# Reordering the last stage of a Fourier-mixing and gated-MLP kernel: kept operands loaded one by one, seven-product units behind other units, another PSUM bank for one block

## The chip, the cores and the metric

The kernel runs on one core of one Trainium2 chip. The metric is the time of one execution on the device in microseconds (us), and lower is better. Engines are named as the profile names them: PE is TensorE (PEld its weight loads), DVE is VectorE, ACT is ScalarE, POOL is GpSimd, SP is SyncE, which here only issues DMA transfers; SPq stands for its queue of such instructions.

## What is computed

Two branches read the same layer-normalised input of 2048 tokens by 640 features, and their outputs are added to the input:

```python
xn = _layernorm(x, axis=-1)
a = einsum("bsd,ed->bse", xn, dft_hid_re);  b = einsum("bsd,ed->bse", xn, dft_hid_im)
A = einsum("ts,bse->bte", dft_seq_re, a) - einsum("ts,bse->bte", dft_seq_im, b)
gate = einsum("bsd,df->bsf", xn, W_gate);   up = einsum("bsd,df->bsf", xn, W_up)
B = einsum("bsf,fd->bsd", gate * (gate > 0) * up, W_down)
return x + A + B
```

The gated branch has 1728 hidden features. All is float32.

## The kernel before

**Numbers.** Each float32 operand is split into a high and a low part, and a product is three matmuls, high by high, high by low, low by high (`mm3`, lines 138 to 140). Splitting (`split`, lines 132 and 133) costs an ACT copy for the high part and a DVE subtraction for the low one.

**Stages.** The sequence transform comes first, then gate and up, and last (`project`, about the final 300 us) the products with the hidden transform's and the down projection's weights, which are summed in the same banks. The change touches this last stage alone.

**The last stage.** The tokens are taken in two halves, q=1 first, then q=0, each of two chunks of 512 columns. Products are arranged as Strassen's seven (with Winograd's sums): B11, T1, T2, B22, T3, T4, B21 are their names. Each runs over seven units (`UNITS`, line 1153): three of the hidden transform (`hid`, blocks 0-1, 2-3, 4), four of the down projection (`f`, and `odd`, the block left over, which is unit 4). B21 has only units 2 and 4. A full unit has two 128-row blocks. T1 to T4 first subtract two raw operands on DVE (line 1267), then split; B11, B22 and B21 split what was loaded. B11, T1, B21 and B22 also split their weights; T2, T3 and T4 load weights that were split earlier (`wparts`). A unit has two outputs (banks `a`, `b` or `c`) and, in B11, T1, B21 and B22, a third: the odd block (`v1`, `v2`, `v3`), all in bank `fixed[4]`. When a product is through its units, `read` lets DVE add the banks to tiles `y` (line 1179), which are stored once all their parts are in.

**A second level.** Seven smaller products (`second_level`, named 1 to 7 and run in the order 1, 2, 5, 6, 3, 7, 4), each over three groups, replace one quarter of the blocks. They are the seven-product units, 21 in all. They read operands that are kept throughout: X of q=1 and Y of q=0, three tiles each (pool `quads`), loaded by `fetch`. Products 5, 6, 7 and 4 first add two kept operands on DVE (`plus`, line 1414). They use banks `fixed[5]`, `[6]` and `[7]`.

**Order.** `todo` is a list of units, each with a load, a preparation, a run and a read. `drive(4, 2)` goes through it: at step i it issues the preparation of unit i-2, the load of unit i, the read of unit i-5 and the run of unit i-4. PE, SP and POOL keep this order; each has one queue, in which an instruction that waits holds up all that follow. ACT and DVE are ordered by a planner when the program is built, at most about three units ahead (`in_turn`). What runs ahead is limited by buffers: three `cb` tiles (split operands, pool `ring2`), five `wt` tiles, four `wr` tiles and twenty `rw` tiles (raw operands). In the kernel before, all kept operands and three `y` tiles are loaded at place 14 of the list (`LOADS_AT`), which is between units 4 and 5 of T1, q=1, and from place 20 on one seven-product unit follows every second unit (`spread`, `SINCE`, `EVERY`).

Of the kernel before, what the change touches and what calls it, by code (L numbers as in the profile page):

```python
# [7 lines left out]
F32 = mybir.dt.float32  # L8
# [4 lines left out]
P = 128  # L13
S, D, F = 2048, 640, 1728
KD = D // P
CH = 512
# [19 lines left out]
B11, B12, B21, B22, T1, T2, T3, T4, X4 = range(9)  # L36
# [24 lines left out]
GROUPS = (("hid", 0, 2, 0), ("f", 0, 2, 2), ("f", 4, 1, 4))  # L61
# [4 lines left out]
def fnet_reglu_kernel(  # L66
# [15 lines left out]
    nc = tc.nc  # L82
# [21 lines left out]
    pqd = [dram_p.tile([2, P, KD, CH], F32, name=f"pq{c}") for c in range(NCHUNK)]  # L104
    hd = [dram_p.tile([NF, P, W2], F32, name=f"hd{q}") for q in range(2)]
# [29 lines left out]
    def mm3(ps, w, m, first, last, more=False):  # L135

        (wh, wl), (mh, ml) = w, m
        nc.tensor.matmul(ps, wh, mh, start=first, stop=False, skip_group_check=more)  # L138
        nc.tensor.matmul(ps, wh, ml, start=False, stop=False, skip_group_check=more)  # L139
        nc.tensor.matmul(ps, wl, mh, start=False, stop=last, skip_group_check=more)  # L140
# [12 lines left out]
    todo = []  # L153
    idle = lambda: None
# [637 lines left out]
    steps = [(q, i) for q in (1,) for i in range(SET_STEPS)]  # L792
# [48 lines left out]
    pool = open_pools.__getitem__  # L841
# [312 lines left out]
    ODD_AT, PARTS = 4, {"T2": Z2, "T3": Z3, "T4": Y22}  # L1154
    UNITS.insert(ODD_AT, ("odd", (0,)))
    SINGLE = (2, ODD_AT)
    LOADS_AT, SINCE, EVERY = 14, 20, 2
    every = range(len(UNITS))
    fixed = [bank() for _ in range(8)]
    y, missing, ends = {}, {}, []  # L1160
# [9 lines left out]
    def get_y(q, *which):  # L1170
        for e, c in which:
            own = f"{q}" if e in (0, 1, 4) and c == 0 else ""
            y[q, e, c] = t = pool("y").tile([P, CH], F32, name=f"y{e}{c}{own}")
            nc.sync.dma_start(t, xt[e * P : (e + 1) * P, (2 * q + c) * CH : (2 * q + c + 1) * CH])
# [18 lines left out]
    def project(q):  # L1193
# [1 line left out]
        raws = {}  # L1195
        A, Bk = (fixed[0:2], fixed[2:4]) if q else (fixed[2:4], fixed[0:2])
        B = {("a", 0): A[0], ("a", 1): A[1], ("b", 0): Bk[0], ("b", 1): Bk[1], ("c", 0): Bk[0], ("c", 1): Bk[1],
             "v1": fixed[4], "v2": fixed[4], "v3": fixed[4]}

        def get(kind, u):  # L1200
            what, ks = UNITS[u]
# [16 lines left out]
        def unit(name, u, first, last):  # L1218
            what, ks = UNITS[u]
# [89 lines left out]
            def run():  # L1309
                b, w = t["b"], t["w"]  # L1310
                key, o, row4 = {"B11": ("a", 0, (2 * P, "v1")), "T1": ("b", P, (0, "v2")), "B21": ("c", 0, (2 * P, "v3")),
                                "T2": ("a", 0, None), "B22": ("b", P, (0, "v2")), "T3": ("a", 0, None),
                                "T4": ("a", 0, None)}[name]
                more = name in ("T2", "B22", "T3", "T4")
                for out, oo in [((key, i), o + i * P) for i in range(2)] + ([(row4[1], row4[0])] if row4 else []):
                    if short:
                        for v in range(2):
                            nc.tensor.matmul(B[out], w[:, v, oo : oo + P], b, start=False, stop=last and v == 1, skip_group_check=more)  # L1318
                        continue
                    if (q, name, u, out) == (0, "T4", len(UNITS) - 1, ("a", 1)):  # L1320


                        add_y(0, 3, 0, B[out])
                        for half in range(2):
                            at, ps = slice(half * HC, (half + 1) * HC), fixed[5 + half][:, :HC]
                            for j in range(n):
                                mm3(ps, (w[:, j, 0, oo : oo + P], w[:, j, 1, oo : oo + P]), (b[:, 0, j, at], b[:, 1, j, at]),
                                    j == 0, j == n - 1)
                            ends.append((ps, half))
                        continue  # L1330
                    for j in range(n):
                        mm3(B[out], (w[:, j, 0, oo : oo + P], w[:, j, 1, oo : oo + P]), (b[:, 0, j], b[:, 1, j]),
                            first and not more and j == 0, last and j == n - 1, more)

            return load, prepare, run

        LOADS_Y = {"B11": ((0, 0), (1, 0), (4, 1), (4, 0)) if q else ((4, 1),), "T1": ((2, 1), (3, 1)), "T2": ((0, 1), (1, 1)), "T4": ((2, 0), (3, 0))}

        def read(name):
            two = range(2)  # L1340
            if name == "B11":
                todo = [(4, 1, "v1"), (4, 0, "v1")] + [(i, 0, ("a", i)) for i in two]
            elif name == "T1":
                todo = [(2 + i, 1, ("b", i)) for i in two]
            elif name == "B21":
                todo = [(i, 0, ("c", i)) for i in two] + [(4, 0, "v3")]
            elif name == "T2":
                todo = [(i, 1, ("a", i)) for i in two]
            elif name == "B22":
                todo = [(i, 1, ("b", i)) for i in two] + [(4, 1, "v2")]  # L1350
            elif name == "T3":
                todo = [(2 + i, 1, ("a", i)) for i in two]
            else:
                todo = [(2 + i, 0, ("a", i)) for i in two]
            for e, c, key in todo:
                if name == "T4" and q == 0 and e == 3:
                    for ps, j in ends:
                        add_y(q, e, c, ps, at=slice(j * HC, (j + 1) * HC), queue=(nc.scalar, nc.sync)[j])
                else:
                    add_y(q, e, c, B[key], late=q == 0 and name in ("T3", "T4"))  # L1360

        steps = []
        for name, us in (("B11", every), ("T1", every), ("T2", every), ("B22", every[:4]), ("T3", every),
                         ("B22", every[4:]), ("T4", every[:2]), ("B21", SINGLE), ("T4", every[2:])):
            whole = SINGLE if name == "B21" else every
            for u in us:
                l, p, r = unit(name, u, u == whole[0], u == whole[-1])
                steps.append((l, p, r, (lambda name: lambda: read(name))(name) if u == whole[-1] else idle))
                if u == (5 if (q, name) == (1, "B11") else 3) and name in LOADS_Y:
                    steps.append(((lambda which: lambda: get_y(q, *which))(LOADS_Y[name]), idle, idle, idle))  # L1370
        return steps

    def second_level():
# [2 lines left out]
        X, Y = {}, {}  # L1376
        a, x, v = fixed[5:]

        def fetch(g):
            what, k, n, _ = GROUPS[g]  # L1380
            for t, q in ((X, 1), (Y, 0)):
                t[g] = o = pool("quads").tile([P, 2 * n, CH], F32, name=f"q{q}{g}")
                if what == "hid":
                    nc.sync.dma_start(o, pqd[2 * q][1][:, k : k + 2 * n])
                else:
                    first = 2 * k + 1
                    nc.sync.dma_start(o, hd[q][first : first + 4 * n - 1 : 2, :, :CH].rearrange("f p t -> p f t"))  # L1387

        def unit(name, g):
            what, k, n, at = GROUPS[g]  # L1390
# [21 lines left out]
            def prepare():  # L1412
                lo, hi = halves
                plus = lambda o, i: nc.vector.tensor_tensor(o, o, i, op=OP.add)
                with in_turn():
                    src = {"1": X[g][:, lo], "2": X[g][:, hi], "5": X[g][:, lo], "6": X[g][:, lo], "3": Y[g][:, hi],
                           "7": Y[g][:, lo], "4": X[g][:, lo]}[name]
                    if name in "5674":
                        plus(src, {"5": Y[g][:, lo], "6": Y[g][:, hi], "7": Y[g][:, hi], "4": X[g][:, hi]}[name])
                    t["b"] = b = pool("ring2").tile([P, 2, SG, CH], F32R, name="cb")[:, :, :n]  # L1420
                    lows.append(split(b[:, 0], b[:, 1], src))
                    if "r" in t:
                        cs = slice(0 if block is not None else P, 2 * P if odd else P)
                        split(t["w"][:, :, 0, cs], t["w"][:, :, 1, cs], t["r"][:, :, cs])
# [16 lines left out]

            return load, prepare, run, read if g == len(GROUPS) - 1 else idle

        loads = [((lambda g: lambda: fetch(g))(g), idle, idle, idle) for g in range(len(GROUPS))]
        loads.append((lambda: get_y(0, (0, 0), (1, 0), (4, 0)), idle, idle, idle))
        return loads, [unit(name, g) for name in "1256374" for g in range(len(GROUPS))]

    def spread(steps, more, since, every_n):

        mixed, more = [], list(more)  # L1450
        for i, s in enumerate(steps):
            mixed.append(s)
            if i >= since and (i - since) % every_n == every_n - 1 and more:
                mixed.append(more.pop(0))
        assert not more, len(more)
        return mixed

    steps = project(1) + project(0)
    loads, quads = second_level()
    steps[LOADS_AT:LOADS_AT] = loads  # L1460
    todo.extend(spread(steps, quads, SINCE, EVERY))
    with tc.manual_schedule(engines={mybir.EngineType.SP, mybir.EngineType.Pool, mybir.EngineType.PE}):
        drive(4, 2)

# [38 lines left out]
```

## Time and profile before

| | us |
|---|---|
| median of three runs | 1039.2 (1038.14 to 1041.25) |
| the profiled execution | 1038.6 |
| its span, first to last instruction | 1036.8 |
| PE busy | 1020.4 |
| DVE busy | 837.1 |
| the three matmuls of `mm3` with `cb` and `wt` | 159.1, 159.3 and 158.8, 407 each |

The profile is of one execution. Its page gives the busy time of each engine, the span in 40 slices of 25.9 us (digits are tenths), the DMA queues, and the costliest groups of instructions. Other views used below: the list of who waited for whom (engine, line, what for; total us, times, longest), instructions in order of time (start, us, engine, line, operation; in brackets the idle time of the engine before and who ended it), windows (busy us and count of PE, PEld, DVE, ACT and POOL, then granted clock, DMA share and GB/s) and groups of instructions by line and shape (busy us, mean ns | idle before). Matmuls overlap, so a row's 0.39 us is not the distance to the next one. Rows of SPq are the issue of a transfer, not its time.

### The profile page before, as it was taken

The numbers are of one execution on the slowest core, as the hardware profiler recorded it, in microseconds if no ns is written. First come the engines' busy times: TensorE is split into PE (matmuls) and PEld (weight loads), VectorE is DVE, ScalarE is ACT, GpSimd is POOL, SyncE is SP. The second block draws the span as 40 slices with busy tenths as digits, with TensorE's granted clock in tenths as the row PEclk, the third lists the DMA queues.
The fourth block names the chain that finished last, engine by engine and source line by source line (L and its number), as shares of the span: only waits on it lengthen the run. The fifth ranks groups of instructions, "written<-read, shape, count | busy, mean of one in ns | idle before, by whom it ended". The sixth has DMA issues, their size and how long they took to land.

```text
span 1036.8 us, 12735 instructions
## 1 busy us (share of the span) xinstructions
PE 1020.4 (98%) x4510; PEld 842.3 (81%) x4510; DVE 837.1 (81%) x1178; ACT 458.5 (44%) x592; POOL 104.7 (10%) x171
## 2 busy tenths in 40 slices
PE   9999999999999999999999999999979999999998
PEld 8888888888888888888888888888867888787886
DVE  7967977969889697787878888885657889989777
ACT  6764453333334444333446444443524445554443
POOL 2000011112200002311100110111000001000001
PEclk9999999999999999999999999999998999999999
DMA  9884744958859566763464667653996586978775
GB/s 331 327 278 158 257 150 137 364 199 266 319 207 368 174 210 223 247 200 132 179 243 156 224 233 266 236 208 123 355 399 224 169 249 187 304 254 270 224 233 179
DMA packets 114767, 245.31 MB, mean 237 GB/s; under 512 B 12688, under 2 KB 63120, under 8 KB 112912
## 3 DMA queue, kind: packets, MB, share of 16 engines
q1 hardware_dynamic: 96320, 171.72, 50.1%
q0 software_dynamic: 17952, 72.36, 18.8%
q8 instruction: 35, 0.57, 0.2%
q10 hardware_dynamic: 432, 0.43, 0.1%
q14 instruction: 28, 0.23, 0.1%
HBM read 185.73 MB, written 57.69 MB: 235 GB/s over the span
## 4 chain that ended last, share of the span: by engine, by line
PE 91%; DMA 4%; DVE 3%; SPq 1%; issue 0%; ACT 0%; ACTq 0%; DVEq 0%
PE ps L140 29%; PE ps L139 29%; PE ps L138 29%; PE ps L526 3%; DMA wr<-in_wd 2%; DMA rw<-hd 1%; DVE cb L133 1%; PE ps L555 1%; DVE rw L1267 1%; DMA rw<-pq 1%; PE ps L1318 1%; PE ps L120 1%; DVE wt L133 0%; DMA ro<-hd 0%; SPq L1387 0%
## 5 line engine op out<-in xcount | busy, mean ns | idle before, releaser
L138 PE MATMUL ps<-cb,wt 128*128 128x512 f32 (+1 forms) x407 | 159.1, 391 | 8.3 <-ACT wt L132 7.6
L139 PE MATMUL ps<-cb,wt 128*128 128x512 f32 (+1 forms) x407 | 159.3, 391 | 3.2 <-DVE cb L133 3.2
L140 PE MATMUL ps<-cb,wt 128*128 128x512 f32 (+1 forms) x407 | 158.8, 390 | 0.1
L132 ACT ACTIVATE cb<-rw 128x1024 fp32r<-128x1024 f32 (+1 forms) x73 | 71.1, 976 | 99.2 <-PE ps L140 56.9
L132 ACT ACTIVATE cb<-raw 128x1024 fp32r<-128x1024 f32 x64 | 67.9, 1060 | 105.2 <-PE ps L140 97.0
L133 DVE TENSOR_TENSOR cb<-rw,cb 128x1024 fp32r<-128x1024 f32 (+1 forms) x73 | 81.5, 1118 | 29.8 <-ACT cb L132 29.5
L133 DVE TENSOR_TENSOR cb<-raw,cb 128x1024 fp32r<-128x1024 f32 x64 | 78.1, 1220 | 31.8 <-ACT cb L132 31.5
L138 PE MATMUL ps<-xs_early,gw 128*128 128x512 f32 x260 | 101.1, 389 | 0.0
L139 PE MATMUL ps<-xs_early,gw 128*128 128x512 f32 x260 | 101.1, 389 | 0.0
L140 PE MATMUL ps<-xs_early,gw 128*128 128x512 f32 x260 | 101.1, 389 | 0.0
L138 PEld LDWEIGHTS ps<-cb,wt 128*128 128x128 f32 x407 | 76.9, 189 | 25.0 <-ACT wt L132 8.1
L139 PEld LDWEIGHTS ps<-cb,wt 128*128 128x128 f32 x407 | 76.9, 189 | 21.1 <-DVE cb L133 5.2
L138 PE MATMUL ps<-cb,xs_late 128*128 128x512 f32 x232 | 90.2, 389 | 0.0
L139 PE MATMUL ps<-cb,xs_late 128*128 128x512 f32 x232 | 90.2, 389 | 0.0
L140 PE MATMUL ps<-cb,xs_late 128*128 128x512 f32 x232 | 90.2, 389 | 0.0
L140 PEld LDWEIGHTS ps<-cb,wt 128*128 128x128 f32 x407 | 76.8, 189 | 16.0 <-DVE wt L133 0.6
L138 PE MATMUL ps<-cb,xs_early 128*128 128x512 f32 x226 | 87.9, 389 | 0.0
L139 PE MATMUL ps<-cb,xs_early 128*128 128x512 f32 x226 | 87.9, 389 | 0.0
L140 PE MATMUL ps<-cb,xs_early 128*128 128x512 f32 x226 | 87.9, 389 | 0.0
L129 ACT ACTIVATE gw<-z 128x1024 fp32r<-128x1024 f32 (+1 forms) x52 | 57.0, 1112 | 36.5 <-PE ps L140 21.0
L129 ACT ACTIVATE u<-ps 128x512 f32<-128x512 f32 x52 | 31.2, 599 | 89.6 <-PE ps L140 77.7
L874 DVE TENSOR_TENSOR gw<-z,gw 128x1024 fp32r<-128x1024 f32 (+1 forms) x52 | 64.7, 1283 | 1.9 <-ACT gw L129 1.8
(208 smaller groups left out, 2034.9 us busy)
## 6 DMA issues: line engine op xcount, KB each, us to landing
raw<-in_dft SPq DMA_DIRECT2D x94, 512.0 KB, 5.6
wt<-wparts SPq DMA_DIRECT2D x70, 256.0 KB, 3.9
z<-in_wgu SPq DMA_DIRECT2D x26, 640.0 KB, 4.1
hd<-ob POOLq DMA_DIRECT2D x26, 512.0 KB, 3.2
wparts<-pw POOLq DMA_DIRECT2D x12, 1024.0 KB, 5.1
rw<-hd SPq DMA_DIRECT2D x24, 512.0 KB, 6.0
tk<-in_dft SPq DMA_DIRECT2D x16, 512.0 KB, 8.3
rw<-pq SPq DMA_DIRECT2D x16, 512.0 KB, 5.0
```

Of the source, the lines that this page charges most:

```text
L120: nc.tensor.matmul(ps[:, :P], warm, warm, start=True, stop=True)
L129: return nc.scalar.activation(o, i, AF.Copy)
L132: nc.scalar.activation(hi, src, AF.Copy)
L133: return nc.vector.tensor_tensor(lo, src, hi.bitcast(F32), op=OP.subtract)
L138: nc.tensor.matmul(ps, wh, mh, start=first, stop=False, skip_group_check=more)
L139: nc.tensor.matmul(ps, wh, ml, start=False, stop=False, skip_group_check=more)
L140: nc.tensor.matmul(ps, wl, mh, start=False, stop=last, skip_group_check=more)
L526: nc.tensor.matmul(E[0, key], xn_part(n * SG + j, d)[v == 1], b[:, int(v == 2), j], start=False, stop=n % NH == NH - 1 and (j, v) == (SG - ...
L555: nc.tensor.matmul(E[c, key], xn_part(j, d)[v == 1], b[c][0][:, int(v == 2), j], start=j == 0 and v == 0, stop=False)
L874: tt(self.w[:, 1, cs], self.z[:, cs], self.w[:, 0, cs].bitcast(F32), op=OP.subtract)
L1267: sub = lambda o, i0, i1: nc.vector.tensor_tensor(o, i0, i1, op=OP.subtract)
L1318: nc.tensor.matmul(B[out], w[:, v, oo : oo + P], b, start=False, stop=last and v == 1, skip_group_check=more)
```

## The change

The order of the last stage is written anew, and one bank moves:

- Kept operands and y tiles: `fetch` loads one tile at a time. The eight loads (X0, X1, X2, one y, Y0, Y1, Y2, two y) come one by one behind units 1, 3, 5 and 6 of T2, units 1, 3 and 5 of T3, and unit 2 of T4, all of q=1.
- The seven-product units stand one behind each unit of B22 of q=1, B11 of q=0 and B22 of q=0, seven each.
- For q=1, `v1` uses `fixed[7]` instead of `fixed[4]`. For q=0 it keeps `fixed[4]`, and the `v2` products of unit 0 of T1 are put behind the first output of unit 1.

```diff
-    LOADS_AT, SINCE, EVERY = 14, 20, 2
...
-             "v1": fixed[4], "v2": fixed[4], "v3": fixed[4]}
+             "v1": fixed[7 if q else 4], "v2": fixed[4], "v3": fixed[4]}
+        put_off = []
...
-                for out, oo in [((key, i), o + i * P) for i in range(2)] + ([(row4[1], row4[0])] if row4 else []):
+                each = [((key, i), o + i * P) for i in range(2)] + ([(row4[1], row4[0])] if row4 else [])
+                if (q, name, u) == (0, "T1", 0):
+                    put_off.append(each.pop())
+                for out, oo in each:
...
+                    if (q, name, u, out) == (0, "T1", 1, ("b", 0)):
+                        begin()
+                if put_off and (q, name, u) == (0, "T1", 0):
+                    out, oo = put_off.pop()
+                    put_off.append(lambda: [mm3(B[out], (w[:, j, 0, oo : oo + P], w[:, j, 1, oo : oo + P]), (b[:, 0, j], b[:, 1, j]),
+                                                j == 0, False) for j in range(n)])
+
+            begin = lambda: put_off.pop()()
...
-                steps.append((l, p, r, (lambda name: lambda: read(name))(name) if u == whole[-1] else idle))
+                step = [(l, p, r, (lambda name: lambda: read(name))(name) if u == whole[-1] else idle)]
                 if u == (5 if (q, name) == (1, "B11") else 3) and name in LOADS_Y:
-                    steps.append(((lambda which: lambda: get_y(q, *which))(LOADS_Y[name]), idle, idle, idle))
+                    step.append(((lambda which: lambda: get_y(q, *which))(LOADS_Y[name]), idle, idle, idle))
+                steps.append((step, (q, name, u)))
...
-        def fetch(g):
+        def fetch(t, q, g):
             what, k, n, _ = GROUPS[g]
-            for t, q in ((X, 1), (Y, 0)):
-                t[g] = o = pool("quads").tile([P, 2 * n, CH], F32, name=f"q{q}{g}")
...
+            t[g] = o = pool("quads").tile([P, 2 * n, CH], F32, name=f"q{q}{g}")
...
-        loads = [((lambda g: lambda: fetch(g))(g), idle, idle, idle) for g in range(len(GROUPS))]
-        loads.append((lambda: get_y(0, (0, 0), (1, 0), (4, 0)), idle, idle, idle))
+        alone = lambda f: (f, idle, idle, idle)
+        loads = [alone((lambda t, q, g: lambda: fetch(t, q, g))(t, q, g)) for t, q in ((X, 1), (Y, 0)) for g in range(len(GROUPS))]
+        loads.insert(3, alone(lambda: get_y(0, (4, 0))))
+        loads.append(alone(lambda: get_y(0, (0, 0), (1, 0))))
...
-    steps = project(1) + project(0)
     loads, quads = second_level()
-    steps[LOADS_AT:LOADS_AT] = loads
-    todo.extend(spread(steps, quads, SINCE, EVERY))
+    LOADS_AFTER = [(1, "T2", u) for u in (1, 3, 5, 6)] + [(1, "T3", u) for u in (1, 3, 5)] + [(1, "T4", 2)]
+    for q in (1, 0):
+        for steps, of in project(q):
+            todo.extend(steps)
+            if of in LOADS_AFTER:
+                todo.append(loads.pop(0))
+            if of[:2] in ((1, "B22"), (0, "B11"), (0, "B22")):
+                todo.append(quads.pop(0))
```

More of the change, by code (lines that the diff above doesn't have):

```diff
@@ L1377, in second_level @@
         a, x, v = fixed[5:]
-        def fetch(g):
+        def fetch(t, q, g):
             what, k, n, _ = GROUPS[g]
-            for t, q in ((X, 1), (Y, 0)):
-                t[g] = o = pool("quads").tile([P, 2 * n, CH], F32, name=f"q{q}{g}")
[L1383 to L1387, printed above, removed]
+            t[g] = o = pool("quads").tile([P, 2 * n, CH], F32, name=f"q{q}{g}")
+            if what == "hid":
+                nc.sync.dma_start(o, pqd[2 * q][1][:, k : k + 2 * n])
+            else:
+                first = 2 * k + 1
+                nc.sync.dma_start(o, hd[q][first : first + 4 * n - 1 : 2, :, :CH].rearrange("f p t -> p f t"))
         def unit(name, g):
@@ L1415, in prepare @@
                 with in_turn():
-                    src = {"1": X[g][:, lo], "2": X[g][:, hi], "5": X[g][:, lo], "6": X[g][:, lo], "3": Y[g][:, hi],
-                           "7": Y[g][:, lo], "4": X[g][:, lo]}[name]
+                    which, half = {"1": (X, lo), "2": (X, hi), "5": (X, lo), "6": (X, lo), "3": (Y, hi), "7": (Y, lo), "4": (X, lo)}[name]
+                    src = which[g][:, half]
                     if name in "5674":
-                        plus(src, {"5": Y[g][:, lo], "6": Y[g][:, hi], "7": Y[g][:, hi], "4": X[g][:, hi]}[name])
+                        which, half = {"5": (Y, lo), "6": (Y, hi), "7": (Y, hi), "4": (X, hi)}[name]
+                        plus(src, which[g][:, half])
                     t["b"] = b = pool("ring2").tile([P, 2, SG, CH], F32R, name="cb")[:, :, :n]
@@ L1442, in unit @@
             return load, prepare, run, read if g == len(GROUPS) - 1 else idle
-        loads = [((lambda g: lambda: fetch(g))(g), idle, idle, idle) for g in range(len(GROUPS))]
-        loads.append((lambda: get_y(0, (0, 0), (1, 0), (4, 0)), idle, idle, idle))
+        alone = lambda f: (f, idle, idle, idle)
+        loads = [alone((lambda t, q, g: lambda: fetch(t, q, g))(t, q, g)) for t, q in ((X, 1), (Y, 0)) for g in range(len(GROUPS))]
+        loads.insert(3, alone(lambda: get_y(0, (4, 0))))
+        loads.append(alone(lambda: get_y(0, (0, 0), (1, 0))))
         return loads, [unit(name, g) for name in "1256374" for g in range(len(GROUPS))]
[L1448 to L1456, printed above, removed]
-    steps = project(1) + project(0)
-    loads, quads = second_level()
-    steps[LOADS_AT:LOADS_AT] = loads
-    todo.extend(spread(steps, quads, SINCE, EVERY))
+    loads, quads = second_level()
+    LOADS_AFTER = [(1, "T2", u) for u in (1, 3, 5, 6)] + [(1, "T3", u) for u in (1, 3, 5)] + [(1, "T4", 2)]
[6 more added lines that the diff above has]
+                todo.append(quads.pop(0))
+    assert not loads and not quads
     with tc.manual_schedule(engines={mybir.EngineType.SP, mybir.EngineType.Pool, mybir.EngineType.PE}):
```

## The prediction

> **What bounds the kernel now.** I read the page first, then what TensorE waited for, then TensorE's instructions in order of time.
>
> ```profile
> span 1036.8 us, 12735 instructions
> ...
> PE 1020.4 (98%) x4510; PEld 842.3 (81%) x4510; DVE 837.1 (81%) x1178; ACT 458.5 (44%) x592; POOL 104.7 (10%) x171
> ...
> PE   9999999999999999999999999999979999999998
> PEclk9999999999999999999999999999998999999999
> ```
>
> TensorE is the bound: 98% busy. One slice, the 31st (777 to 803 us), stands out, and there the granted clock falls too. What it waited for over the whole span:
>
> ```profile
> PE ps L138 <- ACT wt L132: 7.6, 1, 7.6
> PE ps L139 <- DVE cb L133: 3.2, 3, 1.8
> ...
> PE ps L138 <- DVE y L1179: 0.6, 1, 0.6
> ```
>
> So five waits are all that an edit of the order can win. I place them by counting matmuls from 730.11 us, where unit 0 of B11, q=1, begins (18 matmuls for a unit of two blocks and three outputs, 12 for two outputs). Here are the first two of them:
>
> ```profile
> 757.08 0.39 PE L140 MATMUL ps<-cb,wt 128*128 128x512 f32 x1
> 758.09 0.50 PE L138 MATMUL ps<-cb,wt 128*128 128x512 f32 x1 [0.62 <-DVE y L1179]
> ...
> 769.10 0.39 PE L138 MATMUL ps<-cb,wt 128*128 128x512 f32 x1
> ...
> 771.60 0.39 PE L140 MATMUL ps<-cb,wt 128*128 128x512 f32 x1
> 779.62 0.80 PE L138 MATMUL ps<-cb,wt 128*128 128x512 f32 x1 [7.64 <-ACT wt L132]
> ...
> 784.75 0.39 PE L140 MATMUL ps<-cb,wt 128*128 128x512 f32 x1
> ```
>
> Eleven matmuls start from 769.10 to 771.60: 0.227 us each. At 758.09 stands T1, unit 0, third output (`v2`): 1.01 us after the one before, 0.78 lost. At 779.62 stands T1, unit 5. From 771.60 to 784.75 twelve matmuls start in 13.15 us where 2.72 would do: **10.4 us lost**, 7.8 by waiting and 2.6 by slow matmuls:
>
> ```profile
> 770.00:780.00 10.00, 2.36 (x10) 1.60 (x8) 2.36 (x2) 1.79 (x2) 0.00 (x0) 0.71 1.06 390
> 780.00:785.00 5.00, 4.92 (x13) 3.50 (x13) 5.00 (x6) 2.85 (x3) 0.00 (x0) 0.56 1.09 354
> 785.00:790.00 5.00, 5.00 (x24) 4.14 (x23) 4.29 (x6) 1.58 (x2) 0.00 (x0) 1.00 0.19 70
> ```
>
> The granted clock is 0.71, then 0.56, then 1.00 again. The wait is named for ACT, but ACT was itself late. I follow it back through VectorE to the transfers:
>
> ```profile
> 776.46 1.23 DVE L1267 TENSOR_TENSOR rw<-rw 128x1024 f32<-128x1024 f32 x1 [10.06 <-DMA rw<-hd]
> ```
>
> ```profile
> 755.20 1.01 SPq L1384 DMA_DIRECT2D q<-pq  x2
> 756.62 5.92 SPq L1387 DMA_DIRECT2D q<-hd  x4
> 762.59 2.20 SPq L1174 DMA_DIRECT2D y<-in_xt  x3
> 764.83 1.41 SPq L1216 DMA_DIRECT2D rw<-hd  x1
> ```
>
> ```profile
> 754.60:779.60 25.00, 16.76 (x73) 13.24 (x71) 12.62 (x17) 5.89 (x8) 0.00 (x0) 0.89 1.05 399
> ```
>
> The operand of T1, unit 5 (`rw<-hd`, 764.83) is issued behind the six kept operands and three y tiles, and the transfers are full all that time (399 GB/s, last column). The kept operands are four of 1.05 MB and two of 0.52, the y tiles three of 0.26: 6.0 MB, 15.1 us at 399 GB/s.
>
> **Part 1, the kept operands.** All nine transfers remain, but each now follows a unit of T2, T3 or T4. T1, unit 5 then is next in SP's queue at 755.2, and its operand, seen at 776.46, would land 15.1 us sooner, near 761.3. From its landing to the first matmul took 779.62 - 776.46 = 3.2 us; without a wait that matmul is due at 771.83. It must land by 768.6: 7.3 us to spare. So the wait goes, and with it the slow matmuls: **-10.4**.
>
> What is late next? The three operands of q=1 (X: 1.05, 1.05, 0.52 MB) fall into T2, the three of q=0 (Y, same sizes) into T3. The weight slices of both stages wait for one of five `wts` tiles, so SP cannot run far ahead. In T2 the tightest slices, those of unit 4, can go out when unit 0 ends, 6.8 us before they are used (30 matmuls); the operand ahead of them went out some 5 us earlier. Slices land in 3.5 us in the median (this row is of T3, q=0):
>
> ```profile
> wt<-wparts SPq DMA_DIRECT2D x12, 256.0 KB, 3.5
> ```
>
> So some 3 us are left: 0 for T2. T3 is tighter. It appears without extra transfers for q=0:
>
> ```profile
> 986.50:1002.80 16.30, 16.30 (x73) 13.49 (x72) 11.32 (x13) 8.67 (x11) 0.00 (x0) 1.00 0.80 247
> ```
>
> It moves 247 GB/s at a DMA share of 0.80, with TensorE never waiting. In q=1 the slices of T3, unit 1 wait for a tile that is freed 6.8 us before T3 begins; Y0 follows. From there to the end of unit 6's loads stand 6.7 MB: Y 2.6, operands and slices of units 2 to 6 4.1. Unit 6 starts 13.6 us into T3; less some 1.5 us to start a transfer, 17.9 us are there. At 399 GB/s the 6.7 MB take 16.8 us: no wait. At 247/0.80 = 309 GB/s they take 21.7: 3.8 us of wait. I take **+1.0**, nearer the full queue's row, which is the state that this stage would be in, and keep 0 and 3.8.
>
> How a wait is priced hangs on the clock. Two waits below, 1.76 us the longer, leave it at 1.00 in this trace; 7.64 us halved it. The Trainium skill, "TensorE: Matmul & The Clock Gate", section "HAM oscillation — how this bites in real kernels", says that idle gaps beyond about 3.4 us drop the clock and shorter ones don't; the trace agrees on both sides. By that rule a new wait of 3.8 us would cost 6.4, one of 3 us only itself.
>
> **Part 2, the bank.** For q=1 the odd block of B11 (`v1`) goes to bank 7 instead of bank 4, so T1's `v2` need not wait until VectorE has read `v1`: **-0.8**. Bank 7's former tenant is the last result of the gate-and-up rest, read by
>
> ```profile
> 730.94 0.68 DVE L989 TENSOR_TENSOR st<-ps,st 64x512 f32<-64x512 f32 x1 [0.75 <-ACT st L988]
> ```
>
> until 731.62, while `v1`'s first matmul comes 12 after 730.11, at 732.83. 1.2 us cover it; were that read later, each us beyond would be lost again. For q=0 six matmuls move behind the next unit's first six. Their number is unchanged and TensorE doesn't wait there now: 0. They hold one of three `cb` tiles 1.4 us longer; unit 3 begins 4.8 us after even the later release: covered.
>
> **Part 3, the seven-product units.** All 21 are kept, now behind each unit of B22 (q=1), B11 and B22 (q=0). Now they run from T2 of q=1 to T1 of q=0, where VectorE was late twice; a third such wait is in the last stage:
>
> ```profile
> 893.57 0.50 PE L139 MATMUL ps<-cb,wt 128*128 128x512 f32 x1 [1.76 <-DVE cb L133]
> ...
> 941.74 0.50 PE L139 MATMUL ps<-cb,wt 128*128 128x512 f32 x1 [0.92 <-DVE cb L133]
> ...
> 1030.28 0.50 PE L139 MATMUL ps<-cb,wt 128*128 128x512 f32 x1 [0.54 <-DVE cb L133]
> ```
>
> The first is T4, unit 5 of q=1, the second T1, unit 3 of q=0, the third T4, unit 6 of q=0. The first shows why:
>
> ```profile
> 891.16 1.22 DVE L1414 TENSOR_TENSOR q<-q 128x1024 f32<-128x1024 f32 x1
> 892.30 2.35 DVE L133 TENSOR_TENSOR cb<-rw,cb 128x1024 fp32r<-128x1024 f32 x2
> ```
>
> A sum for a seven-product unit stood ahead of the `cb` that TensorE needed. With no such unit among T1 to T4 both go: **-2.7**. T4 of q=1 then looks like T4 of q=0, which has none now and still waits: **+0.6** (0.54 and its restart; 0 to 1.8).
>
> But the units with the most sums (products 6, 7, 4) now meet B11 and B22 of q=0. The prices:
>
> ```profile
> L133 DVE TENSOR_TENSOR cb<-rw,cb 128x1024 fp32r<-128x1024 f32 x59 | 71.8, 1220 | 24.5 <-ACT cb L132 24.3
> ...
> L133 DVE TENSOR_TENSOR wt<-wr,wt 128x768 fp32r<-128x768 f32 x29 | 27.6, 951 | 1.9 <-ACT wt L132 1.9
> ...
> L133 DVE TENSOR_TENSOR cb<-q,cb 128x1024 fp32r<-128x1024 f32 x14 | 17.1, 1220 | 1.4 <-ACT cb L132 1.3
> ...
> L133 DVE TENSOR_TENSOR cb<-q,cb 128x512 fp32r<-128x512 f32 x7 | 4.8, 687 | 1.0 <-ACT cb L132 1.0
> ...
> L1414 DVE TENSOR_TENSOR q<-q 128x1024 f32<-128x1024 f32 x4 | 4.9, 1217 | 0.0
> ```
>
> A B11 or B22 unit costs VectorE 1.22 + 0.95 = 2.2 us for 4.1 of TensorE. Product 6 or 7 costs 1.22 + 1.22 = 2.4 for 1.4 (6 matmuls). Together 4.6 for 5.5: that fits. The crowded place is product 4 behind the last three units of B22, q=0:
>
> ```profile
> 1002.90:1021.20 18.30, 18.30 (x82) 15.16 (x81) 17.16 (x22) 7.61 (x10) 1.62 (x3) 1.00 0.68 208
> ```
>
> There VectorE has 1.1 us idle in 18.3 already. Product 4 adds about two units of 2.4 and one of 1.4, with small weight splits 7 us, for 15 matmuls, 3.4 us. That is 3.6 more work than time; less the idle 1.1, 2.5 late. T3 just before it has VectorE 5 us idle (11.32 of 16.30, quoted above), but work may be taken at most some three units ahead. Between 0 and 2.5, and with the last T4 losing its lead up to 3: **+1.5**.
>
> The sum: -10.4 - 0.8 - 2.7 + 1.0 + 0.6 + 1.5 = -10.8. The profiled execution took 1038.6 us (1036.8 of span, 1.8 around it), so 1027.8. It lies 0.6 under the median of the runs, 1039.2; I write **1028**.
>
> **Rivals.** (1) *The transfers' wait moves to T3 of q=1.* For it: 6.7 MB in 17.9 us need 374 GB/s, and T3's many 256 KB slices have not run at more than 247 on the mean. Against it: that stage was not full there, and full stretches show 399. At 309 GB/s 3.8 us and the halved clock's 2.6 take the place of my 1.0, at 285 5.6 and 2.6: 1033 to 1035. (2) *VectorE becomes the bound around q=0's B11 and B22.* For it: product 4's 2.5 us, and the order of VectorE's work is fixed beforehand, so that a wrong turn such as that at 891.16 costs 1 to 2 us wherever it falls. Against it: B11 and B22 leave it 1.9 us per unit. With the full 3 at the end and the 2.7 back in other places: 1032. (3) *The change doesn't do what it says*: T1, unit 5 is late even without the nine transfers, since transfers are full from 734 us on. Against it: 7.3 us to spare. With half of the 10.4 left: 1033. (4) *Slower:* rival 1's mechanism, at its extreme. Every transfer of SP is in one order, so Y in T3 delays the slices of all later units. It decides from 220 GB/s: then 6.7 MB take 30.4 us, 12.5 of wait and 2.6 of clock, which eat the 11.8 gained elsewhere and 3 more: 1042. Nothing seen in a full stretch is so low.
>
> **How the numbers follow.** Forecast 0.70, rival 1 0.14, rival 2 0.08, rival 3 0.05, rival 4 0.03. The forecast's own ends: no wait in T3, none new in the last stage, none in T4 of q=1 give 1024.7; a little less if the last stage's own wait shrinks too, 1024.3. All three at their bounds (3.8, 3 and 1.8) give 1033.3. I take 1024.3 to 1033.5, which also holds part of rivals 1 to 3. 0.3% is 3.1 us, about what a measurement of this kernel can tell from no change: faster 0.92, within 0.05, slower 0.03, since rivals 1 to 3 mostly stay beyond 3.1.
>
> **What would show it.** Right: T1, unit 5 without a wait, and the clock at 1.00 through the slice of 777 us; no wait on `y` at T1, unit 0; no wait at T1 of q=0. Wrong: a TensorE wait named for a slice (`wt`) or a DMA in T3 of q=1; VectorE without idle time and `cb` waits over 2 us after B22 of q=0; a wait in B11, unit 0 of q=1 for bank 7. If the clock falls anywhere, the forecast is too low.

## The result, and the profile after

| | before | after |
|---|---|---|
| median, us | 1039.82 (five runs, 1038.14 to 1041.38) | 1034.83 (five runs, 1034.15 to 1035.23) |
| the profiled execution, us | 1038.6 | 1035.23 |
| its span, us | 1036.8 | 1033.5 |

The ratio is 0.995, with a 95% interval of 0.9935 to 0.9964: faster by 5.0 us. The forecast was 1028.0, in a range of 1024.3 to 1033.5. The direction was right, about half of the gain came, and the time lies 1.3 us above the range.

The page of the changed kernel: span, the engines' busy time, and the 40 slices of TensorE and of its granted clock.

```profile
span 1033.5 us, 12722 instructions
...
PE 1020.2 (99%) x4510; PEld 840.5 (81%) x4510; DVE 837.8 (81%) x1178; ACT 457.5 (44%) x592; POOL 104.8 (10%) x171
...
PE   9999999999999999999999999999999989999997
...
PEclk9999999999999999999999999999999999999999
```

Both dips of before are gone: TensorE's own, which stood in the 30th slice (752 to 778 us) and not in the 31st as the prediction reads it, and the clock's in the 31st. A slight new one stands in the 33rd (827 to 853 us). What TensorE waited for (what for, who, total us, times, longest):

```profile
PE ps L139 <- DVE cb L133: 2.9, 5, 0.9
PE ps L138 <- DMA wt<-wparts: 2.1, 3, 1.5
PE ps L1321 <- DVE wt L133: 2.1, 2, 1.4
PE ps L140 <- DVE wt L133: 1.4, 1, 1.4
PE ps L120 <- DVE warm L116: 1.1, 1, 1.1
```

The one wait of 7.6 us has become many short ones, none above 1.5 us. The last row is the start of the program and was there before. Their places, from TensorE's instructions in order of time:

```profile
797.92 0.50 PE L140 MATMUL ps<-cb,wt 128*128 128x512 f32 x1 [1.35 <-DVE wt L133]
...
831.43 0.47 PE L138 MATMUL ps<-cb,wt 128*128 128x512 f32 x1 [0.35 <-DMA wt<-wparts]
...
833.30 0.47 PE L138 MATMUL ps<-cb,wt 128*128 128x512 f32 x1 [0.25 <-DMA wt<-wparts]
...
837.80 0.47 PE L138 MATMUL ps<-cb,wt 128*128 128x512 f32 x1 [1.51 <-DMA wt<-wparts]
...
842.17 0.74 PE L1321 MATMUL ps<-cb,wt 128*128 128x512 f32 x2 [1.37 <-DVE wt L133]
...
904.11 0.50 PE L139 MATMUL ps<-cb,wt 128*128 128x512 f32 x1 [0.77 <-DVE cb L133]
...
1018.69 0.50 PE L139 MATMUL ps<-cb,wt 128*128 128x512 f32 x1 [0.88 <-DVE cb L133]
...
1022.20 1.15 PE L1321 MATMUL ps<-cb,wt 128*128 128x512 f32 x4 [0.72 <-DVE wt L133]
...
1026.93 0.50 PE L139 MATMUL ps<-cb,wt 128*128 128x512 f32 x1 [0.56 <-DVE cb L133]
```

The first is B22, unit 0 of q=1, then T3, units 4, 5 and 6 of q=1, and B22, unit 4 of q=1; 904.11 is B11, unit 5 of q=0, and the last three are T4, units 3, 4 and 6 of q=0. Each wait costs a little more than its idle time, because the next matmuls start late too. So I add up, as the prediction did, what each start-to-start distance has over 0.227 us (those above 0.30 us):

| place in the last stage | before, us lost | forecast | after, us lost |
|---|---|---|---|
| T1, unit 0 of q=1 (the bank) | 0.9 | 0 | 0 |
| T1, unit 5 of q=1 (the transfers) | 10.4 | 0 | 0 |
| T2, unit 4, and B22, unit 0, of q=1 | 0 | 0 | 0.2 + 1.6 |
| T3, units 4 to 6 of q=1 | 0 | 1.0 | 2.8 |
| B22, unit 4 of q=1 | 0 | 0 | 1.6 |
| T4 of q=1 | 2.0 | 0.6 | 1.0 |
| B11, unit 5 of q=0 | 0 | 0 | 1.1 |
| T1, unit 3 of q=0 | 1.2 | 0 | 0 |
| B22, unit 5, and T4, of q=0 | 1.1 | 2.6 | 0.45 + 2.95 |
| sum, before rounding | 15.7 | 4.2 | 11.8 |

With what is lost in the earlier stages the sums over the whole program are 16.1 and 12.4, a difference of 3.7 where the two profiled executions differ by 3.4. The medians differ by 5.0: the profiled execution of before lay 1.2 us under its median here, that of after 0.4 above its own. Those 1.6 us are between executions and have no place in a trace.

### The profile page after: what moved, and what is told of

Same layout as the page of the kernel before. It is cut to its first block, busy times and chain, and to the rows that moved or that the text cites. A ratio compares the mean times of both kernels' runs of the same rounds, so it can differ in the third digit from the quotient of the medians.

```text
span 1033.5 us, 12722 instructions
## 1 busy us (share of the span) xinstructions
PE 1020.2 (99%) x4510; PEld 840.5 (81%) x4510; DVE 837.8 (81%) x1178; ACT 457.5 (44%) x592; POOL 104.8 (10%) x171
## 4 chain that ended last, share of the span: by engine, by line
PE 91%; DVE 4%; DMA 4%; ACT 1%; issue 0%; SPq 0%; ACTq 0%
PE ps L139 29%; PE ps L140 29%; PE ps L138 29%; PE ps L526 3%; DVE cb L133 1%; DMA wt<-wparts 1%; DMA q<-hd 1%; DVE rw L1267 1%; PE ps L555 1%; DVE y L1178 1%; ACT cb L132 1%; DVE wt L133 1%; DMA wr<-in_hid 1%; PE ps L120 1%; DMA wr<-in_wd 0%
```

## The experiments

**The theories.** (A) What was lost is due to where the kept operands now load: in T2 and T3 they delay weight slices and weights. (B) What was lost is due to where the seven-product units now stand: VectorE is short of time there. (C) The transfers are slow because of their shape, long rows from a queue that has run empty. (D) Within A, part of the loss is VectorE's fixed order, not the transfers themselves. Four experiments tell A from B, one C, one D, and two look at the bank and at the put-off products.

### e1_bank: the bank alone

The kernel before, with this one edit:

```diff
-             "v1": fixed[4], "v2": fixed[4], "v3": fixed[4]}
+             "v1": fixed[7 if q else 4], "v2": fixed[4], "v3": fixed[4]}
```

> The kernel before with one edit: v1 of q=1 in bank 7. If the 0.8 us at T1, unit 0 were a wait for the bank alone, that wait is gone, the wait of unit 5 of T1 is as long as before, and the time is 0.5 to 1 us under the kernel before (1038 to 1039). If another wait stood behind it (an operand, a split), the loss stays and the time is that of before.

One execution took 1040.34 us, the kernel before 1040.48 (median) on the same chip. In the list of TensorE's waits the row for `y` (0.6 before) is gone, and no matmul of T1, unit 0 starts late. The big wait stays, here 7.9 us. So the bank does what it says. What that is worth in time isn't resolved: this trace lost 17.7 us over the whole program against 16.1 before, with 11.5 instead of 10.4 at T1, unit 5, and a new 0.9 at B22, unit 5, of q=1 (862.09 us). VectorE's order comes out anew with each edit, which may be why small waits move; that is not shown here.

### e2_bulk: parts 2 and 3 without part 1

All eight loads go back between units 4 and 5 of T1, in the order of before (X0, Y0, X1, Y1, X2, Y2, then the y tiles); the rest is the changed kernel.

```diff
-            if of in LOADS_AFTER:
-                todo.append(loads.pop(0))
+            if of == (1, "T1", 4):
+                todo.extend(loads)
+                loads = []
```

> The changed kernel, but with all kept operands and y tiles loaded at once between units 4 and 5 of T1, as before. Theory (the one-by-one loads make the waits that are new in T2, T3 and in the units of B22 behind them, 6.3 us by the trace): these go, the 10.4 us at T1, unit 5 come back: 1038 to 1040. Rival (T2 and T3 ask more of the transfers than they can give as soon as no seven-product unit stands between their units): the 6.3 us stay, 1044 to 1046.

1039.96 us against 1040.48, ratio 0.9994 (0.9984 to 1.0004). Its own waits and windows:

```profile
PE ps L138 <- ACT wt L132: 8.1, 1, 8.1
PE ps L139 <- DVE cb L133: 2.3, 4, 1.0
PE ps L1321 <- DVE wt L133: 1.5, 2, 0.8
```

```profile
770.00:780.00 10.00, 2.19 (x10) 1.49 (x8) 1.74 (x2) 1.60 (x2) 0.00 (x0) 0.73 1.06 389
780.00:785.00 5.00, 4.69 (x10) 3.24 (x11) 5.00 (x6) 3.04 (x4) 0.00 (x0) 0.53 1.08 372
```

The wait of T1, unit 5 is back, with the clock at 0.73 and then 0.53 (the column after POOL's). All waits of T2, T3 and of B22's units 0 and 4 are gone: they come with the places of the loads, as theory A has it (how, at B22, e8 shows). The waits in the two T4 stay: they belong to part 3. So the measured price of each part is this. Parts 2 and 3 together bring 0.06% (-0.6 us, from -1.7 to +0.4) where I had -1.4 (-0.8 - 2.7 + 0.6 + 1.5). Part 1 brings the rest, from 0.9994 to 0.995, some 4.6 us, where I had 9.4 (-10.4 + 1.0). Most of the error is in part 1.

### e3_y_b22 and e4_xy: the loads in other places

e3 takes Y and the last two y tiles out of T3 and T4 and puts them behind the first units of B22, q=1; e4 also has X earlier and more loads in B22. The first line is e3's, the second e4's:

```diff
+    LOADS_AFTER = [(1, "T2", u) for u in (1, 3, 5, 6)] + [(1, "B22", u) for u in (0, 1, 2, 3)]
...
+    LOADS_AFTER = [(1, "T2", 0), (1, "T2", 2)] + [(1, "B22", u) for u in range(6)]
```

> The changed kernel with Y0, Y1, Y2 and the two y tiles behind units 0 to 3 of B22, q=1, instead of T3 and T4. Theory (Y in front of T3's slices makes T3's 2.8 us and the 1.6 us of unit 4 of B22): both go, 1030 to 1031. Rival (T3 by itself is too dense): no change beyond 1 us, 1034 to 1035. If Y then delays the weights of B22 instead, a wait for weights shows in B22 and the gain is smaller.

> As the last one, and X too goes elsewhere: X0 behind unit 0 of T2, X1 behind unit 2, X2, one y, Y0 and Y1 behind units 0 to 3 of B22, Y2 and two y behind its units 4 and 5. Theory (the full queue of T2 makes the 0.2 us in T2 and the 1.6 us at unit 0 of B22): both go as well, 1028 to 1029.5. Rival (unit 0 of B22 waits for VectorE, not for its weights): they stay, 1030 to 1031.

e3: 1029.14 us (1028.95 to 1030.19) against 1040.48, ratio 0.9893 (0.9872 to 0.9915). e4: 1028.6 us (1027.42 to 1029.81), ratio 0.9887 (0.986 to 0.9913). Both intervals lie wholly below that of the changed kernel. In e3, the window in which T3's loads ran in the changed kernel, and TensorE's one wait from 795 to 845 us:

```profile
816.80:838.40 21.60, 21.60 (x97) 17.87 (x96) 16.67 (x19) 10.38 (x14) 0.00 (x0) 1.00 0.77 244
```

```profile
797.42 0.50 PE L140 MATMUL ps<-cb,wt 128*128 128x512 f32 x1 [1.35 <-DVE wt L133]
```

TensorE is busy in all 21.6 us and the transfers have room (share 0.77). With Y moved, both the slices' waits in T3 and the wait at B22, unit 4 go; the 1.35 at B22, unit 0 stays, and goes only in e4 (0.16 idle). The loads' places, with nothing else touched, thus decide about 6 us (1028.6 against 1034.83).

### e5_repack: the seven-product units spread out, on top of e4

The 21 units begin earlier: two behind some units of B22 (q=1) and one unit of B11, and only four behind B22 of q=0.

```diff
+    BEHIND = {(1, "B22", u): n for u, n in enumerate((1, 2, 1, 2, 1, 1, 1))}
+    BEHIND.update({(0, "B11", u): n for u, n in enumerate((1, 1, 1, 2, 1, 1, 1))})
+    BEHIND.update({(0, "B22", u): 1 for u in range(4)})
...
-            if of[:2] in ((1, "B22"), (0, "B11"), (0, "B22")):
+            for _ in range(BEHIND.get(of, 0)):
                 todo.append(quads.pop(0))
```

> The loads of e4_xy, and the 21 seven-product units moved forward so that none stands behind the last three units of B22, q=0: nine behind B22 of q=1, eight behind B11 of q=0, four behind units 0 to 3 of B22, q=0. Theory (product 4 behind the last units of B22 leaves VectorE late in the last T4): the last stage's waits fall from 2.4 us (three places) to the 1.1 us of the kernel before, 1.0 to 1.5 us less than e4_xy: about 1027.3. Rival (these waits come from T4's own short units): they stay at 2.4 us, and the time at that of e4_xy, 1028.6. The 1.0 us at unit 5 of B11, q=0, may go too if it came from product 6 beside it, another 1 us.

1027.79 us (1026.24 to 1028.28) against 1039.86, ratio 0.9883 (0.9868 to 0.9897). This version beats both kernels. Its span and engines on the page, then all that TensorE waited for:

```profile
span 1025.9 us, 12732 instructions
...
PE 1018.4 (99%) x4510; PEld 840.1 (82%) x4510; DVE 837.4 (82%) x1178; ACT 458.2 (45%) x592; POOL 105.0 (10%) x171
```

```profile
PE ps L139 <- DVE cb L133: 1.1, 2, 0.6
PE ps L120 <- DVE warm L116: 1.1, 1, 1.1
PE ps L1321 <- DVE wt L133: 0.8, 2, 0.4
PE ps L555 <- ACT xs_early L257: 0.6, 1, 0.6
PE ps L140 <- DVE wt L133: 0.2, 1, 0.2
```

The last T4 loses 1.4 us instead of e4's 2.7, by the rule of the table above. So theory B holds there: product 4 behind the last units of B22 was part of the last stage's loss. B11, unit 5 no longer waits either (1.1 lost in e4), but this doesn't show that the units beside it were the cause: in e2, e7 and e8, which have the same units there as the changed kernel, it lost only 0.1 to 0.3. In time, e4 and e5 can't be told apart (their intervals overlap); the traces tell them apart.

### e6_split_fetch: the long rows cut

The changed kernel, with each 1 MB fetch of a `hid` operand issued as four of 256 KB.

```diff
-                nc.sync.dma_start(o, pqd[2 * q][1][:, k : k + 2 * n])
+                for j in range(2 * n):
+                    nc.sync.dma_start(o[:, j], pqd[2 * q][1][:, k + j])
```

> The changed kernel, with the hidden transform's kept operands (X0 and Y0, 1 MB each) fetched as four transfers of 256 KB, rows of 2 KB instead of 8 KB. In the changed kernel such a transfer took 5.6 us of the queue, where 2.6 us were reckoned. Theory (the long rows move slowly when the queue was empty before): it takes 2.6 to 3.2 us, T3 waits 1 to 2.5 us less, 1032 to 1033.5. Rival (the pace is that of the memory after a pause, whatever the rows): unchanged, 1034 to 1035.5.

1033.10 us (1032.41 to 1035.22) against 1039.86, ratio 0.994 (0.992 to 0.996): not told apart from the changed kernel. By the landings in the trace Y0 held the queue from 816.88 to 820.88 us, 4.0 us, against 5.6 in the changed kernel (816.79, when the transfer ahead of it landed, to 822.43), X0 4.4 against 5.8. That lies between the theories: at 399 GB/s 1.05 MB take 2.6 us. T3 lost 1.8 us instead of 2.8. But theory C's other half, the empty queue, doesn't stand up against the other runs. Uncut, with 8 KB rows, X0 and Y0 took 2.5 us each in the kernel before, Y0 in e3 2.5 behind a full queue (share 1.06 in the 4 us before) and Y0 in e4 2.6 behind a half-empty one (0.58). X0 in e4 took 4.5 although the queue was full before it (0.96). All that took 4.5 us or more stood among the loads of T2 or T3, all that took 3.2 or less stood in T1 or B22. TensorE in order of time:

```profile
797.85 0.50 PE L140 MATMUL ps<-cb,wt 128*128 128x512 f32 x1 [1.36 <-DVE wt L133]
...
835.89 0.47 PE L138 MATMUL ps<-cb,wt 128*128 128x512 f32 x1 [0.78 <-DMA wt<-wparts]
...
837.32 0.50 PE L138 MATMUL ps<-cb,wt 128*128 128x512 f32 x1 [0.50 <-DMA wt<-wparts]
...
841.04 1.66 PE L1321 MATMUL ps<-cb,wt 128*128 128x512 f32 x6 [1.37 <-DVE wt L133]
```

The telling row is the first. The weights of B22, unit 0 landed at 793.09 us instead of 794.60, with T2 ending at the same time within 0.1, yet the wait is the same to 0.01 us as in the changed kernel, 1.36 against 1.35. A wait that hangs on a landing would hardly repeat like that. It points at something fixed. The last row repeats too (1.37), but tells less, since there T3's end and the weights both moved forward by 1.1 us.

### e7_no_putoff: `v2` of T1, unit 0, q=0 not put off

```diff
-                if (q, name, u) == (0, "T1", 0):
-                    put_off.append(each.pop())
...
-                    if (q, name, u, out) == (0, "T1", 1, ("b", 0)):
-                        begin()
```

> The changed kernel without the putting off: for q=0, v2 of T1, unit 0, runs in its own unit again. Theory (put off or not, TensorE does the same and has waited for nothing there, since a seven-product unit now stands between): no wait at that place, within 0.3% of the changed kernel, 1034 to 1035.5. Rival (bank 4 would still be unread): a wait of up to 0.9 us at T1, unit 0, q=0.

1034.65 us (1033.57 to 1036.85) against 1039.86, ratio 0.9954 (0.9936 to 0.9972), as the changed kernel. T1 of q=0 has no wait either way: the put-off is worth nothing.

### e8_adds_later: VectorE's adds behind the splits

What is fixed, by the theory, is VectorE's order. In the changed kernel, around TensorE's starts at 797.92 and 842.17:

```profile
794.58 1.23 DVE L133 TENSOR_TENSOR cb<-q,cb 128x1024 fp32r<-128x1024 f32 x1 [1.10 <-ACT cb L132]
795.72 1.28 DVE L1178 TENSOR_TENSOR y<-ps,y 128x512 f32<-128x512 f32 x2
796.92 0.95 DVE L133 TENSOR_TENSOR wt<-wr,wt 128x768 fp32r<-128x768 f32 x1
...
839.46 0.69 DVE L1178 TENSOR_TENSOR y<-ps,y 128x512 f32<-128x512 f32 x1 [0.83 <-PE ps L140]
840.07 0.54 DVE L133 TENSOR_TENSOR wt<-wr,wt 64x384 fp32r<-64x384 f32 x1
840.84 0.69 DVE L1178 TENSOR_TENSOR y<-ps,y 128x512 f32<-128x512 f32 x1 [0.22 <-PE ps L140]
841.56 0.56 DVE L133 TENSOR_TENSOR wt<-wr,wt 64x384 fp32r<-64x384 f32 x1
```

The adds to `y` read the banks of T2 and of T3, so each must follow TensorE's last matmul into its bank, and they stand ahead of the weight split which TensorE needs for its next unit. At unit 4 the add waits for TensorE, the split for the add, and TensorE for the split: at 839.46 and at 840.84 the brackets show it (idle, ended by TensorE). At unit 0 the adds didn't wait (795.72 has no bracket); there it is their own 1.28 us, ahead of the split at 796.92. e8 orders the adds behind the split, for q=1 alone:

```diff
+                elif q and name in ("T2", "T3"):
+                    with tc.issue_after(late[q, "B22", 0 if name == "T2" else 4].ins):
+                        add_y(q, e, c, B[key])
```

Here `late` holds the weight split of B22, unit 0 or unit 4.

> The changed kernel, its loads and units untouched; only the adds that read T2 and T3 of q=1 out of their banks are put behind VectorE's weight split for the next unit (units 0 and 4 of B22). Theory (the 1.5 us at unit 0 and the 1.5 us at unit 4 of B22 are VectorE's fixed order: adds that wait for the end of T2 or T3 stand ahead of the split): both fall under 0.4 us, T3's waits for slices (2.8 us) stay, 1031.5 to 1033. Rival (the weights themselves land too late): both stay above 1 us, 1034 to 1035.5.

1032.94 us (1032.55 to 1033.9) against 1039.54, ratio 0.9939 (0.9922 to 0.9956). VectorE, then TensorE, at B22, unit 0:

```profile
795.10 0.95 DVE L133 TENSOR_TENSOR wt<-wr,wt 128x768 fp32r<-128x768 f32 x1
795.97 0.68 DVE L1178 TENSOR_TENSOR y<-ps,y 128x512 f32<-128x512 f32 x1
```

```profile
796.11 0.50 PE L140 MATMUL ps<-cb,wt 128*128 128x512 f32 x1 [0.16 <-DVE wt L133]
```

The split is first, and the wait falls from 1.35 to 0.16 us. In time e8 can't be told from the changed kernel (the intervals overlap); its trace can. At B22, unit 4 the loss falls from 1.6 to 0.1, but the small unit behind it now loses 1.4, waiting for its own weights' split (0.20 and 0.61 idle). Theory D holds at both places, and at the second most of it is given back a few matmuls later. T3's loss stays, as D says; it even grows, from 2.8 to 3.5. Of the 2.5 us that e8's trace loses less in all, these places with T3 and the small unit make 0.75; most of the rest lies at B11, unit 5 and in the last T4, which the edit doesn't touch. So the time fell into the theory's range partly by luck; the rows, not the time, bear the theory out.

The order also tells why other places for the loads remove the two waits. In e4, at B22, unit 0, VectorE has the split first:

```profile
795.26 0.95 DVE L133 TENSOR_TENSOR wt<-wr,wt 128x768 fp32r<-128x768 f32 x1
796.13 1.28 DVE L1178 TENSOR_TENSOR y<-ps,y 128x512 f32<-128x512 f32 x2
```

In e3 the two splits of unit 4 begin at 833.74 us, and T3's first add comes at 838.41. That the weights of unit 4 land late is not what costs the time: the last of them landed 1.3 us before T3's last matmul in the changed kernel (839.13 against 840.41) and in e8 alike (837.96 against 839.23), and only the order differs.

### All runs beside each other

The losses over the whole program, by the same rule, against the time of the profiled execution. They count from the first matmul that isn't one of the warm-up's; it starts between 6.0 and 6.2 us in all ten, so e5's 0.6 us for `xs_early`, a wait that ends there, isn't counted, nor its like in e1 and e3:

| kernel | lost, us | profiled execution, us | without the loss |
|---|---|---|---|
| before | 16.1 | 1038.6 | 1022.5 |
| e1_bank | 17.7 | 1040.34 | 1022.6 |
| e2_bulk | 18.2 | 1041.12 | 1022.9 |
| after | 12.4 | 1035.23 | 1022.8 |
| e7_no_putoff | 12.2 | 1035.15 | 1022.9 |
| e6_split_fetch | 10.4 | 1033.43 | 1023.0 |
| e8_adds_later | 9.9 | 1032.55 | 1022.7 |
| e3_y_b22 | 7.6 | 1030.19 | 1022.6 |
| e4_xy | 5.8 | 1028.45 | 1022.6 |
| e5_repack | 4.9 | 1027.67 | 1022.8 |

The last column holds within 0.5 us while the times span 13.5. TensorE's late starts are, within that 0.5 us, the whole difference between these profiled executions.

## Why the prediction was half right

**What came as forecast.** The wait of T1, unit 5 went with its slow matmuls (-10.4), the bank's wait went (-0.9 against -0.8), and the two waits of T4 and T1 behind seven-product sums went (-2.7, or 3.2 with the late starts behind them, less the 1.0 that T4 of q=1 still loses, against 0.6). The granted clock, taken slice by slice, stood at 1.00, with waits up to 1.51 us. The rule cited from the Trainium skill, "TensorE: Matmul & The Clock Gate", section "HAM oscillation — how this bites in real kernels", that short gaps leave the clock alone, agrees with that and with e2, where 8.05 us lowered it to 0.53. No run has a wait between 1.76 us and 7.64, so its 3.4 us itself isn't tested here.

**The step that failed first: T3, "I take +1.0, nearer the full queue's row".** The sum was right in kind, so many MB in so much time, but the rate was wrong, and so was a small step before it: its terms, 6.8 + 13.6 - 1.5, make 18.9 us, not the 17.9 that it goes on with. The stretch of T3's loads in the changed kernel, from Y0's first packets to the last slice of unit 6 (T3's own matmuls start at 821.40), as a whole and then cut where Y0 has landed:

```profile
816.80:838.40 21.60, 19.49 (x85) 15.19 (x83) 14.46 (x16) 7.20 (x8) 0.00 (x0) 1.00 0.98 327
816.80:822.40 5.60, 5.60 (x27) 4.62 (x26) 5.60 (x8) 1.70 (x2) 0.00 (x0) 1.00 0.88 278
822.40:838.40 16.00, 13.89 (x60) 10.56 (x58) 8.86 (x9) 5.50 (x6) 0.00 (x0) 1.00 1.01 344
```

The queue was full (0.98) and moved 327 GB/s, not 399. By the landings, the 6.7 MB themselves took 21.6 us (816.79 to 838.37), which is 310 GB/s; the 327 hold some later transfers as well. I had the better row in hand: T3 of q=0, 247 GB/s at a share of 0.80, gives 309. At that the 6.7 MB take 21.7 us, 3.8 over the 17.9 written and 2.8 over the 18.9 that the terms make; T3 lost 2.8. That the last two agree to a tenth is in part luck: the slices of unit 1 went out 8.0 us before T3 began (813.43), not 6.8. I took the other row because its state, a full queue, was the same, but its packets were not. The transfers' view has the packets, for the full stretch before (754.6 to 779.6 us) and for T3 after (816.8 to 838.4 us):

```profile
DMA packets 5159, 9.97 MB, mean 399 GB/s; under 512 B 360, under 2 KB 1704, under 8 KB 4902
```

```profile
DMA packets 4898, 7.06 MB, mean 327 GB/s; under 512 B 336, under 2 KB 3047, under 8 KB 4775
```

A third of the packets were under 2 KB in the first, 62% in the second. Grouped by size in the trace:

| packet, bytes | full stretch before: count, mean ns | T3 after: count, mean ns |
|---|---|---|
| 512 | 649, 27 | 535, 28 |
| 1024 | 695, 46 | 2176, 50 |
| 2048 | 3070, 86 | 1728, 93 |
| 8192 | 256, 312 | 121, 397 |

With the first column's durations T3's mix (and 336 packets of 4 bytes, 9 ns each) would take 304 us of packets, 19.0 us on 16 engines: 371 GB/s. So the mix explains 399 to 371, and packets that took longer than their kind did before (the 8 KB ones by a quarter, all within the first 5.6 us) explain 371 to 327. Why they took longer isn't settled. e6 says that cutting the 8 KB rows helps somewhat, 4.0 us for Y0 instead of 5.6, but the same uncut rows took 2.5 us elsewhere, so their length alone isn't the cause either. Nor was T3's wait one gap: it came in three, 0.35, 0.25 and 1.51 us, where the prediction would let a wait of 3.8 lower the clock.

**The step that was missing: "0 for T2", and nothing at all for B22's units 0 and 4.** I asked whether the weight slices of T2 would land in time, and they nearly did (0.2 lost). I didn't ask in which order VectorE would meet what landed. The loss of 1.6 + 1.6 us at B22's units 0 and 4 is the order read off above: e6 shows at unit 0 that it doesn't follow the landing of the weights, e8 at both that it goes with the order. Rival 2 names this mechanism ("a wrong turn costs 1 to 2 us wherever it falls"), but I looked for it only around the seven-product units, and counted it as a rival at 0.08 instead of a term. That moving the loads (e3, e4) removes the same two waits goes with the order too: the split stands first in both. That the planner chose so because the order is planned anew for each list of units is argued, not shown.

**The mis-sized terms of part 3.** "+1.5" for the last stage: T4 of q=0 and B22, unit 5 lost 3.4 us where before T4 lost 1.1, so +2.3, inside the bound of 3. And "that fits" for products 6 and 7 beside a full unit was 0 against 1.1 at B11, unit 5 of q=0. There VectorE wasn't short of time; ACT was late first, then VectorE behind it, as ACT's and VectorE's instructions show:

```profile
900.27 0.85 ACT L132 ACTIVATE wt<-wr 128x768 fp32r<-128x768 f32 x1 [0.57 <-DMA wr<-in_wd]
901.42 0.42 ACT L132 ACTIVATE wt<-wr 128x256 fp32r<-128x256 f32 x1 [0.31 <-DMA wr<-in_hid]
901.75 1.04 ACT L132 ACTIVATE cb<-rw 128x1024 fp32r<-128x1024 f32 x1
```

```profile
902.83 1.23 DVE L133 TENSOR_TENSOR cb<-rw,cb 128x1024 fp32r<-128x1024 f32 x1 [0.38 <-ACT cb L132]
```

ACT's order put two weight splits, whose weights came late, ahead of the `cb` that TensorE needed at 903.1. So what this execution shows is an arrival and an order, and not my sum of durations, 4.6 of VectorE beside 5.5 of TensorE. The wait differs between kernels that don't touch the place (0.8 idle here, 0.5 in e6, none in e8), which fits; no run tests it alone.

**The rivals.** Rival 1, the transfers' wait in T3 with 1033 to 1035 us, gives the measured time and has the right place, but not the right parts: 2.8 of wait in T3 and 1.6 behind it instead of 3.8 and 2.6 of lowered clock. I gave it 0.14; by the row of T3 of q=0 its wait should have been in the forecast. Rival 3 is out (the 10.4 went whole), and so is rival 4 (327 GB/s, not 220).

## What to carry to other kernels

- To judge whether transfers fit into a stage, take the rate from that stage's own row, scaled to a full share (247 / 0.80 = 309 against 310 by the landings), and not from a full stretch with larger packets (399).
- Where a list of work is rewritten and engines run in a fixed order, check at each seam which instruction stands ahead of the one that TensorE needs next: here adds of a product just ended stood ahead of the split for the next one, 1.6 us lost each time, and no count of busy time shows it.
- A prefetch needs a place, not only an earlier or later time: the same 6 MB cost 10.4 us in T1, some 6 in T2 and T3 with what hung on it, and nearly nothing in e4, with six of the eight loads behind units of B22, where the queue had room (a share of 0.54 in the changed kernel, 797.2 to 816.8 us).

## What the hardware showed beyond this

- The median packet of each size took 27 ns (512 bytes), 46 (1024), 84 (2048), 159 (4096) and 309 (8192), in the full stretch before. From the ends, (309 - 27) / 7680 = 0.0367 ns per byte and, as an estimate, 8 ns for any packet; 4-byte packets took 9. Sixteen engines at 0.0367 ns per byte make 436 GB/s, which is what the Trainium skill, "DMA: Bandwidth & Descriptors", section "Where 436 GB/s comes from", works out for the ports (435.2): the trace agrees.
- The time that one fetch of 1 MB with 8 KB rows held the queue, from the landing ahead of it to its own, ran from 2.5 us (X0 and Y0 in the kernel before) to 6.2 (X0 in e7); in the changed kernel, where X0 took 5.8 and Y0 5.6, single packets took up to 1.7 us. It doesn't follow how full the queue was: 4.5 us for X0 in e4 behind a share of 0.96, 2.6 for Y0 in e4 behind 0.58. What it does follow is open.
